# Layer norm row sums on GpSimd, a new order of the pieces, and a one-lane last pass, in a kernel of two interleaved attention layers

## The chip, the cores and the metric

The kernel runs on one core of one Trainium2 chip. The metric is device time in microseconds (us), the median of several executions; lower is better. Engines are named as in the profile: PE is TensorE's matmuls, PEld its weight loads, DVE is VectorE, ACT is ScalarE, POOL is GpSimd, SP is the engine whose queue issues the weight DMAs.

## The reference

Four residual blocks over 2048 rows of width 640: a recurrent attention layer with memory (A), a local dilated attention layer (B), and both once more with the same weights. Each takes a layer norm of its input.

```
x = x + A(layernorm(x))       # 64 segments of 32 rows, 8 memory rows carried from one to the next
x = x + B(layernorm(x))       # each row attends to 8 rows, two apart
x = x + A(layernorm(x))
x = x + B(layernorm(x))

def A(x):                     # 32 heads of 192
    for s in segments:
        h = concat(mem, x[s])                  # 8 + 32 rows
        q, k, v = h@Wq, h@Wk, h@Wv
        o = (softmax(mask(q k^T / sqrt(192))) v) @ Wo
        mem, out[s] = o[:8], o[8:]
```

## The kernel before

The rows lie in the free dimension, the 640 features in 5 chunks of 128 partitions. The four blocks run as one pipeline: in step t the first A layer works on segment t (lane 0) and the second A layer on segment t-2 (lane 1). Both use the same weights, so a full step has 2 x 40 = 80 columns in each A matmul and 2 x 32 = 64 in each B matmul. There are 66 A steps, of which the first two and the last two have one lane, and a last pass of B alone. `ORDER` lists the pieces of a step; each piece's instructions go to their engines in this order. Capital letters are layer A (K3: the k projection of head group 3; KE3: its eviction; S, E, EM, PO, R, OT: scores, exponential, mask, attention product, reciprocal, normalised output; Oa3, Ob3: output projection halves), small ones layer B, and `L...` the norm for the next step. 79 of the 128 weight pieces stay on chip; 49 are streamed in each step, from a ring of 8 buffers.

```python
ORDER = """
K0 Q0 bsq K0y QE0 KE0 V0 bst bmv VE0 Q1 S0 ... br bap ...
... OT15 E7 OT25 LSQ PO6 EM7 Oa2 R6 T7 Ob2 Oa3 TE7
Ob3 OT16 OT26 Oa5 PO7 Oa6 R7 lst LMV Ob5 Oa4 Ob6 OT17 LR OT27 Ob4 LAP O7x O7y MEMa O7z MEMb X1
"""                                            # [most of it cut]
LAST = "bsq bst bmv br bap bq bqE bk bkE bs0 be0 bv bs1 be1 eb0 bvE bt eb1 btE bp0 on0 bp1 on1 bo boE by byE"

def ln_sq(self, x):                            # bsq, LSQ: sums over the 5 chunks
    nc.vector.tensor_tensor(out=sq, in0=x, in1=x, op=mult)
    for j, v in enumerate((x, sq)):            # 128x64 <- 128x320, twice
        nc.vector.tensor_reduce(out=s[:, j, :], in_=v.rearrange("p c n -> p n c"), op=add, axis=X)
    nc.vector.tensor_copy(out=hl[:, 0], in_=s)                   # high part, bf16
    nc.vector.tensor_tensor(out=hl[:, 1], in0=s, in1=hl[:, 0], op=subtract)   # low part

def ln_stats(self, hl):                        # bst, lst: sum over the partitions by a ones matmul
    for j in range(2): nc.tensor.matmul(ps, lhsT=ones, rhs=hl[:, j], ...)
# ln_mv (bmv, LMV): mean and variance on DVE; ln_r (br, LR): 1/sqrt as exp(-0.5 ln) on ACT

def ln_big(self, x, mr, dst):                  # bap, LAP
    nc.vector.tensor_tensor(out=xc, in0=x, in1=m, op=subtract)   # 128x320
    for l in range(2):
        nc.vector.tensor_tensor(out=dst[:, :, l, :], in0=xc[lane l], in1=r[lane l], op=mult)

def mem_out(self, t, g):                       # MEMa, MEMb: memory rows from PSUM to the next step's input
    nc.vector.tensor_copy(out=h[..., 0:NM], in_=acc_lanes(g)[..., 0:NM])

def b_x1(self, b):                             # X1: x + A(...), from PSUM, in two halves
    nc.vector.tensor_tensor(out=x1, in0=acc, in1=xin, op=add)
# x_take: GpSimd copies the next segment's rows into xin
```

The softmax here doesn't subtract the row's maximum and nothing guards it: scores larger than these inputs give would overflow.

Of the kernel before, what the change touches and what calls it, by code (L numbers as in the profile page):

```python
# [11 lines left out]
F32 = mybir.dt.float32  # L12
ACT = mybir.ActivationFunctionType
# [4 lines left out]
P = 128  # L18
# [26 lines left out]


ORDER = """
K0 Q0 bsq K0y QE0 KE0 V0 bst bmv VE0 Q1 S0 K1 T0 QE1 br bap E0 TE0 KE1 V1 S1 EM0 Q3 PO0 VE1 QE3 E1 bq T1 R0 K2
KE2 bqE TE1 Q2 K3 V2 QE2 OT10 S2 KE3 bk EM1 OT20 S3 PO1 VE2 E2 bkE Q4 T2 EM2 bs1 E3 QE4 V3 R1 K4 TE2 be1 VE3
Q5 OT11 OT21 KE4 PO2 R2 EM3 T3 eb1 bs0 be0 V4 QE5 Oa0 VE4 bv TE3 OT12 OT22 bvE Q6 S4 PO3 eb0 E4 bt R3 QE6 btE  # L50
K5 T4 EM4 K6 KE5 TE4 bp0 V5 OT13 Ob0 OT23 KE6 on0 S5 bp1 VE5 PO4 T5 Oa1 E5 R4 on1 TE5 V6 bo Q7 EM5 OT14 S6 boE
OT24 VE6 Ob1 E6 QE7 PO5 T6 EM6 TE6 by byE R5 K7 KE7 V7 S7 VE7 OT15 E7 OT25 LSQ PO6 EM7 Oa2 R6 T7 Ob2 Oa3 TE7
Ob3 OT16 OT26 Oa5 PO7 Oa6 R7 lst LMV Ob5 Oa4 Ob6 OT17 LR OT27 Ob4 LAP O7x O7y MEMa O7z MEMb X1
""".split()


LAST = """
bsq bst bmv br bap bq bqE bk bkE bs0 be0 bv bs1 be1 eb0 bvE bt eb1 btE bp0 on0 bp1 on1 bo boE by byE
""".split()

def half_order():

    order = []
    for n in ORDER:
        if n[0] in "KQV" and len(n) == 2:
            order += [(n[0].lower(), int(n[1]), 0), (n[0].lower(), int(n[1]), 1)]
        elif n[:2] in ("Oa", "Ob"):
            order.append(("o", int(n[2]), int(n[1] == "b")))
        elif n == "O7x":
            order += [("o", 7, 0), ("o", 7, 1)]  # L70
    assert len(set(order)) == len(order) == 8 * NQUAD
    return order

def half_blocks(kind, i, h):

    if kind == "o":
        if i == NQUAD - 1:
            blocks = [(m, c) for c in range(NC) for m in O_ROWS[0] + O_ROWS[1]]
        else:
            blocks = [(m, c) for rows in O_ROWS for m in rows for c in range(NC)]  # L80
    elif (kind, i) == ("k", 0):
        blocks = [(c, n) for c in range(NC - 1) for n in range(6)] + [(NC - 1, n) for n in range(6)]
    else:
        blocks = [(c, n) for n in range(6) for c in range(NC)]
    return blocks[15 * h:15 * (h + 1)]
# [4 lines left out]
def resident_pieces():  # L90

    at, t = {}, 0.0
    for n in ORDER:
        if n[0] in "KQV" and len(n) == 2 and n != "K0":
            at.update({(n[0].lower(), int(n[1]), h): t + 15 * h for h in range(2)})
        elif n == "K0":
            at.update({("k", 0, h): t + 15 * h for h in range(2)})
        elif n[:2] in ("Oa", "Ob"):
            at[("o", int(n[2]), int(n[1] == "b"))] = t
        elif n == "O7x":  # L100
            at.update({("o", 7, h): t + 15 * h for h in range(2)})
        t += 30 if len(n) == 2 and n[0] in "KQV" else 15 if n[0] == "O" and n[1] in "ab" else 30 if n == "O7x" else NO_WEIGHTS.get(n.rstrip("01234567"), 0)
    pieces = [(at[u] + 8 * q, u + (q,)) for u in half_order() for q in range(2)]
    pieces.sort()
    stream, n_s = set(), len(pieces) - N_RES
    k = 0
    for j in range(n_s):
        want = (j + 0.5) * t / n_s
        while k < len(pieces) - (n_s - j) and abs(pieces[k + 1][0] - want) <= abs(pieces[k][0] - want):
            k += 1  # L110
        stream.add(pieces[k][1])
        k += 1
    return {u for _, u in pieces} - stream

class Kernel:
    def __init__(self, ctx, tc, xT, m0T, wA, wqkv, wo, out):

        self.tc = tc
        self.nc = tc.nc
        self.x = xT  # L120
        self.mem0 = m0T
        self.wA = wA
        self.b_src = (wqkv, wo)
        self.out = out
        self.n_seg = 2 * xT.shape[0]
        pool = lambda name, bufs, **kw: ctx.enter_context(tc.tile_pool(name=name, bufs=bufs, **kw))
        self.cp = pool("consts", 1)
        self.wres = pool("wres", 1)
        self.wring = pool("wring", RING)
        self.ap1 = pool("act1", 1)  # L130
        self.ap2 = pool("act2", 2)
        self.bp = pool("bact", 1)
        self.xp = pool("xio", 1)
        self.ps_one = pool("ps_one", 1, space=PSUM)
        self.units = {}
        self.place = {u: n for n, u in enumerate(half_order())}
        self.resident = resident_pieces()
        self.cur = {}
        self.n_big = 0
        self.xt, self.ots, self.qxs, self.kp, self.qp, self.vp, self.tp = {}, {}, {}, {}, {}, {}, {}  # L140
        self.x_load(0)
        self.build_consts()
# [148 lines left out]
    def span_of(self, t):  # L291

        self.l0 = 0 if t < self.n_seg else 1
        self.l1 = 2 if t >= LAG else 1
        self.cs = slice(LT * self.l0, LT * self.l1)

    def proj(self, ps, kind, i, h, t, chained=False):

# [131 lines left out]
    def a_o7(self, part):  # L430

        for k in {"x": range(18), "y": range(18, 24), "z": range(24, 30)}[part]:
            self.o_mm(NQUAD - 1, k // 15, k % 15)

    def acc_lanes(self, g):

        return self.acc[g][:, 0:(3 - g) * NT].rearrange("p (c l n) -> p c l n", l=2, n=LT)
# [18 lines left out]
    def ln_sq(self, x):  # L456

        nc = self.nc
        sq = self.bp.tile([P, NC, NX], BF16, name="sq", tag="sq")
        nc.vector.tensor_tensor(out=sq[:], in0=x[:], in1=x[:], op=ALU.mult)  # L460
        s = self.bp.tile([P, 2, NX], F32, name="ln_s", tag="xc")
        for j, v in enumerate((x, sq)):
            nc.vector.tensor_reduce(out=s[:, j, :], in_=v[:].rearrange("p c n -> p n c"), op=ALU.add, axis=mybir.AxisListType.X)
        hl = sq[:].rearrange("p c n -> p (c n)")[:, 0:4 * NX].rearrange("p (j a n) -> p j a n", j=2, a=2)
        nc.vector.tensor_copy(out=hl[:, 0], in_=s[:])
        nc.vector.tensor_tensor(out=hl[:, 1], in0=s[:], in1=hl[:, 0], op=ALU.subtract)
        return hl

    def ln_stats(self, hl):
        nc = self.nc  # L470
        ps = self.big("ps_st")
        for j in range(2):
            nc.tensor.matmul(ps[:, 0:2 * NX], lhsT=self.ones[:], rhs=hl[:, j].rearrange("p a n -> p (a n)"), start=(j == 0), stop=(j == 1))  # L473
        return ps

    def ln_mv(self, ps):

        nc = self.nc
        m = self.bp.tile([P, NX], F32, name="ln_m")
        nc.vector.tensor_scalar(out=m[:], in0=ps[:, 0:NX], scalar1=1.0 / D, scalar2=None, op0=ALU.mult)  # L480
        v = self.bp.tile([P, NX], F32, name="ln_v")
        nc.vector.tensor_tensor(out=v[:], in0=m[:], in1=m[:], op=ALU.mult)
        nc.vector.scalar_tensor_tensor(out=v[:], in0=ps[:, NX:2 * NX], scalar=1.0 / D, in1=v[:], op0=ALU.mult, op1=ALU.subtract)
        return m, v

    def ln_r(self, mv):

        nc = self.nc
        m, v = mv
        nc.scalar.activation(out=v[:], in_=v[:], func=ACT.Ln, bias=self.eps_t[:])  # L490
        r = self.bp.tile([P, NX], F32, name="ln_r")
        nc.scalar.activation(out=r[:], in_=v[:], func=ACT.Exp, scale=-0.5)
        return m, r

    def ln_big(self, x, mr, dst):
# [1 line left out]
        nc = self.nc  # L497
        m, r = mr
        xc = self.bp.tile([P, NC, NX], F32, name="ln_xc", tag="xc")
        nc.vector.tensor_tensor(out=xc[:], in0=x[:], in1=m[:].unsqueeze(1).to_broadcast([P, NC, NX]), op=ALU.subtract)  # L500
        for l in range(2):
            nc.vector.tensor_tensor(out=dst[:, :, l, :], in0=xc[:, :, SEG * l:SEG * (l + 1)],
                                    in1=r[:, SEG * l:SEG * (l + 1)].unsqueeze(1).to_broadcast([P, NC, SEG]), op=ALU.mult)

# [22 lines left out]
    def b_kE(self, b):  # L527

        o = SEG * (b % 2)
        for l in range(2):  # L530
            k = self.bkp[:, 0:NC * NX].rearrange("p (c l n) -> p l c n", c=NC, l=2)[:, l]
            self.nc.vector.tensor_tensor(out=self.KX[:, :, l, :, o:o + SEG], in0=k.unsqueeze(2).to_broadcast([P, NC, 2, SEG]),
                                         in1=self.par_mask[:].unsqueeze(3).to_broadcast([P, NC, 2, SEG]), op=ALU.mult)
# [1 line left out]
    def b_qE(self):  # L535

        self.qx = self.bp.tile([P, NC, BPC, NX], BF16, name="QX", tag="xc")
        q = self.bqp[:, 0:NC * NX].rearrange("p (c n) -> p c n", c=NC)
        self.nc.vector.tensor_tensor(out=self.qx[:], in0=q.unsqueeze(2).to_broadcast([P, NC, BPC, NX]),
                                     in1=self.pair_mask[:].unsqueeze(3).to_broadcast([P, NC, BPC, NX]), op=ALU.mult)  # L540

    def b_v(self):
        nc = self.nc
# [195 lines left out]
    def a_piece(self, n, t):  # L739
        if n == "K0":  # L740
            return self.k0(t)
        if n == "K0y":
            return self.k0y()
        if n[:2] == "O7":
            return self.a_o7(n[2])
        if n == "X1":
            return self.b_x1(t)
        k, i = n[:-1], int(n[-1])
# [12 lines left out]
    def step(self, t):  # L761
# [3 lines left out]
        nt = t + 1  # L765
        if a:
            self.span_of(t)
        if 1 < nt < self.n_seg:
            self.x_take(nt)
        for n in ORDER if a else LAST:  # L770
# [82 lines left out]
```

## Time and profile before

| | before |
|---|---|
| time, median of 3 | 3138.72 us (3137.41 to 3142.72) |
| profiled span | 3138.8 us |
| PE busy | 3063.2 us, 98% |
| DVE, ACT, POOL busy | 75%, 56%, 2% |
| median step, row-sum matmul of B's norm to the next step's | 46.44 us |
| first x1 addition of the last rows to the end ("tail") | 21.15 us |

The timeline of the kernel before shows one boundary between two steps: start, length, engine, source line, operation, tiles, shapes, count, and in brackets how long the engine had been idle and what ended that.

```profile
1488.27 0.47 ACT L390 ACTIVATE R<-R 128x320 f32<-128x320 f32 x1
...
1488.78 0.49 DVE L408 TENSOR_TENSOR OT<-ps_o,R 128x320 bf16<-128x320 f32 x1
...
1489.18 0.31 DVE L413 TENSOR_TENSOR OT<-ps_o,R 64x160 bf16<-64x160 f32 x1
...
1489.50 0.32 DVE L414 TENSOR_TENSOR OT<-ps_o,R 64x160 bf16<-64x160 f32 x1
...
1489.85 0.49 DVE L500 TENSOR_TENSOR ln_xc<-xin_88,ln_m 128x320 f32<-128x320 bf16 x1
...
1490.45 0.56 DVE L502 TENSOR_TENSOR hT_92<-ln_xc,ln_r 128x160 bf16<-128x160 f32 x2
...
1490.74 0.42 PE L420 MATMUL ps_acc_49872<-OT,w_o_11_1962 128*128 128x80 bf16 x7
1490.93 0.20 DVE L454 CAST hT_92<-ps_acc_49871 128x48 bf16<-128x48 f32 x1
1491.18 0.45 PE L303 MATMUL ps_k<-hT_92,w_k_00_386 128*128 128x80 bf16 x8
...
1491.97 0.42 POOL L655 COPY xin_86<-XT_49165 128x160 bf16<-128x160 bf16 x1 [46.01 <-DVE x_369 L510]
...
1492.12 0.71 DVE L463 TENSOR_REDUCE ln_s<-x_369 128x64 f32<-128x320 bf16 x1
```

Seven output matmuls start at 1490.74; at 36 ns each the eighth place would be 1490.99, and the first K matmul starts at 1491.18, 0.19 us late. No idle time is shown for it, because the modelled length of a matmul (about 0.2 us here) covers such a wait. It can only be found from the starts. Behind it stands a serial chain on DVE with no gap over 0.11 us: OT products, the norm's subtraction and multiplications, and the copy of the memory rows.

### The profile page before, as it was taken

What the parts mean: (1) busy time and instruction counts of PE and PEld (TensorE: products, weight loads), DVE (VectorE), ACT (ScalarE), POOL (GpSimd) and SP (SyncE); (2) the same over time, 40 slices, a digit from 0 to 9 for tenths busy, and PEclk for the clock granted to TensorE, in tenths of its full rate; (3) what the DMA queues carried; (4) which work ended last, traced back from release to release, by engine and by line L of the source; (5) the groups of instructions that cost most, each with busy time, mean ns of one, the idle gap of its engine ahead of it and who ended that gap; (6) DMA issues with size and microseconds to landing.
All of it is one profiled execution on the core that took longest, in us unless ns stands there. A gap on an engine that the chain in (4) does not pass through costs nothing.

```text
span 3138.8 us, 185804 instructions
## 1 busy us (share of the span) xinstructions
PE 3063.2 (98%) x83160; PEld 3036.4 (97%) x83160; DVE 2358.2 (75%) x6883; ACT 1747.2 (56%) x3829; POOL 48.2 (2%) x162
## 2 busy tenths in 40 slices
PE   6899999999999999999999999999999999999996
PEld 5799999999999999999999999999999999999996
DVE  3577777777777777777777777777777777777775
ACT  2355556555556556556555655555655655655653
POOL 2000000000000000000000000000000000000000
PEclk6899999999999999999999999999999999999998
DMA  9988888888888888888888888888888888888885
GB/s 360 320 263 267 263 262 265 264 264 265 266 268 263 268 266 263 268 266 263 268 266 261 267 263 267 261 265 268 263 267 266 264 267 267 263 269 266 262 274 184
DMA packets 487807, 838.02 MB, mean 267 GB/s; under 512 B 54240, under 2 KB 261984, under 8 KB 487008
## 3 DMA queue, kind: packets, MB, share of 16 engines
q1 hardware_dynamic: 477648, 820.89, 83.2%
q8 instruction: 651, 10.67, 1.4%
q10 hardware_dynamic: 9360, 5.26, 0.6%
q14 instruction: 148, 1.21, 0.1%
HBM read 823.31 MB, written 2.62 MB: 263 GB/s over the span
## 4 chain that ended last, share of the span: by engine, by line
PE 95%; DMA 3%; issue 1%; DVE 1%; ACT 0%; SPq 0%; DVEq 0%; ACTq 0%
PE ps_k L303 18%; PE ps_q L303 18%; PE ps_v L303 18%; PE ps_vt L349 6%; PE ps_o L401 5%; PE ps_s L368 5%; PE ps_by L634 2%; PE ps_bq L523 2%; PE ps_bv L548 2%; PE ps_bk L523 2%; DMA w_ring<-in_wA_dram 1%; PE ps_bs L575 1%; PE ps_bo L598 1%; PE ps_bvt L561 1%; PE ps_st L473 0%
## 5 line engine op out<-in xcount | busy, mean ns | idle before, releaser
L303 PEld LDWEIGHTS <-w_ring 128*128 128x128 bf16 x17754 | 784.4, 100 | 19.4 <-DMA w_ring<-in_wA_dram 10.5
L388 ACT ACTIVATE R<-ps_o 64x320 f32<-64x320 f32 (+1 forms) x1056 | 448.5, 425 | 273.8 <-PE ps_o L401 223.6
L342 ACT CAST VT_140<-ps_v 128x480 bf16<-128x480 f32 (+1 forms) x528 | 288.9, 547 | 230.7 <-PE ps_v L303 227.6
L329 ACT CAST KF_121<-ps_k 128x480 bf16<-128x480 f32 (+1 forms) x264 | 144.1, 546 | 391.2 <-PE ps_k L303 383.3
L374 ACT ACTIVATE Em<-ps_s 80x320 bf16<-80x320 f32 (+1 forms) x528 | 223.3, 423 | 157.2 <-PE ps_s L368 110.7
L420 PEld LDWEIGHTS <-w_ring 128*128 128x128 bf16 x6600 | 291.2, 100 | 3.5 <-DMA w_ring<-in_wA_dram 2.6
L335 DVE CAST QT_127<-ps_q 128x320 bf16<-128x320 f32 (+1 forms) x264 | 127.1, 481 | 203.4 <-PE ps_q L303 203.4
L357 DVE COPY Vt_134<-ps_vt 80x512 bf16<-80x512 bf16 x528 | 219.2, 415 | 71.5 <-PE ps_vt L349 69.3
L349 PE MATMUL ps_vt<-ident,VT_140 128*128 128x128 bf16 x3168 | 267.7, 221 | 0.0
L408 DVE TENSOR_TENSOR OT<-ps_o,R 128x320 bf16<-128x320 f32 (+1 forms) x528 | 249.9, 473 | 22.3 <-ACT R L390 16.6
L329 ACT CAST KF_123<-ps_k 128x480 bf16<-128x480 f32 (+1 forms) x264 | 144.1, 546 | 205.6 <-PE ps_k L303 203.9
L390 ACT ACTIVATE R<-R 128x320 f32<-128x320 f32 (+1 forms) x528 | 244.0, 462 | 16.6
L401 PE MATMUL ps_o<-Em,Vt_134 80*128 80x80 bf16 (+1 forms) x4224 | 238.0, 199 | 1.4 <-issue 1.3
L335 DVE CAST QT_125<-ps_q 128x320 bf16<-128x320 f32 (+1 forms) x264 | 126.5, 479 | 143.1 <-PE ps_q L303 71.9
L349 PEld LDWEIGHTS <-VT_140 128*128 128x128 bf16 x3168 | 191.5, 99 | 0.1
L303 PE MATMUL ps_q<-hT_92,w_ring 128*128 128x80 bf16 (+1 forms) x3234 | 185.8, 201 | 3.7 <-DMA w_ring<-in_wA_dram 2.6
L303 PE MATMUL ps_q<-hT_90,w_ring 128*128 128x80 bf16 (+1 forms) x3234 | 186.3, 201 | 2.2 <-DMA w_ring<-in_wA_dram 1.5
L401 PEld LDWEIGHTS <-Vt_134 80*128 80x128 bf16 x4224 | 181.6, 98 | 1.0 <-issue 0.7
L303 PE MATMUL ps_k<-hT_90,w_ring 128*128 128x80 bf16 (+1 forms) x3003 | 172.7, 201 | 1.4 <-DMA w_ring<-in_wA_dram 0.7
L303 PE MATMUL ps_k<-hT_92,w_ring 128*128 128x80 bf16 (+1 forms) x3003 | 171.8, 201 | 1.4 <-issue 1.4
L380 DVE TENSOR_TENSOR Em<-Em,maskA 80x320 bf16<-80x320 bf16 (+1 forms) x528 | 163.2, 309 | 12.5 <-ACT Em L374 8.4
L414 DVE TENSOR_TENSOR OT<-ps_o,R 64x160 bf16<-64x160 f32 (+1 forms) x528 | 165.1, 313 | 7.3
(3084 smaller groups left out, 8305.2 us busy)
## 6 DMA issues: line engine op xcount, KB each, us to landing
w_ring<-in_wA_dram SPq DMA_DIRECT2D x1716, 256.0 KB, 3.9
w_ring<-in_wA_dram SPq DMA_DIRECT2D x1518, 224.0 KB, 4.0
out_dram<-YT_94 ACTq DMA_DIRECT2D x32, 80.0 KB, 3.7
wqkv_sb<-in_wqkv_dram SPq DMA_DIRECT2D x3, 800.0 KB, 7.7
wo_sb<-in_wo_dram SPq DMA_DIRECT2D x1, 800.0 KB, 7.4
w_k_00_386<-in_wA_dram SPq DMA_DIRECT2D x1, 256.0 KB, 2.8
w_k_10_405<-in_wA_dram SPq DMA_DIRECT2D x1, 256.0 KB, 3.8
w_q_10_438<-in_wA_dram SPq DMA_DIRECT2D x1, 256.0 KB, 4.6
```

Of the source, the lines that this page charges most:

```text
L303: self.nc.tensor.matmul(ps[:, NT * n + c0:NT * n + c1], lhsT=self.block(kind, i, h, k), rhs=hT[:, NT * c + c0:NT * c + c1], start=(h == 0 ...
L329: self.nc.scalar.copy(out=kf[:, :, self.cs], in_=self.kp[i][:, 0:6 * NT].rearrange("p (a n) -> p a n", a=6)[:, :, self.cs])
L335: nc.vector.tensor_copy(out=qt[:, :, 0:4:3, cs], in_=pv[:, :, 0:3:2, cs])
L342: self.nc.scalar.copy(out=vt[:, :, self.cs], in_=self.vp[i][:, 0:6 * NT].rearrange("p (a n) -> p a n", a=6)[:, :, self.cs])
L349: nc.tensor.transpose(out=ps[:, n, :], in_=self.VT[:, NT * n:NT * n + P], identity=self.ident[:])
L357: nc.vector.tensor_copy(out=vt[:, :, 0:4:3, :], in_=src[:, :, 0:3:2, :])
L374: self.nc.scalar.activation(out=e[0:NT, :, cs], in_=self.sv[i][0:NT, :, cs], func=ACT.Exp, scale=float(DH) ** -0.5)
L388: self.nc.scalar.activation(out=r[rows, :, :, self.cs], in_=d, func=ACT.Ln)
L390: self.nc.scalar.activation(out=rf, in_=rf, func=ACT.Exp, scale=-1.0)
L401: nc.tensor.matmul(ov[:, pr, b, self.cs], lhsT=vt[0:NT, 512 * pr + P * b:512 * pr + P * (b + 1)], rhs=em[0:NT, 2 * pr + b // 2, self.cs], ...
L408: self.nc.vector.tensor_tensor(out=ot[:, :, 0:3:2, cs], in0=self.ov[:, :, 0:4:3, cs], in1=self.r[i][:, :, :, cs], op=ALU.mult)
L420: self.nc.tensor.matmul(self.acc[c // 3][:, o:o + self.cs.stop - self.cs.start], lhsT=self.block("o", i, h, k), rhs=ot[:, m, self.cs], sta ...
```

## The change

The intent: take one of the two reductions of each norm off DVE, by three adds on GpSimd; move pieces in the step, above all the last output chunks; and let the last pass of B, in which only lane 1 has rows left, work on that lane alone. The core of the diff; not shown are the same cut to `[:, ns]` in the other norm functions, and small helpers for the new pieces `O6x`, `O6y`:

```diff
 ORDER = """            # [cut]
-K0 Q0 bsq K0y QE0 KE0 V0 bst bmv VE0 Q1 S0 K1 T0 QE1 br bap E0 ...
-... Ob3 OT16 OT26 Oa5 PO7 Oa6 R7 lst LMV Ob5 Oa4 Ob6 OT17 LR OT27 Ob4 LAP O7x O7y MEMa O7z MEMb X1
+K0 K0y Q0 KE0 bsq V0 bst K1 QE0 S0 VE0 Q1 E0 KE1 bmv EM0 ...
+... OT15 OT25 PO6 Oa2 LSQ T7 Ob2 R6 EM7 Oa5 Oa3
+TE7 OT16 OT26 Ob3 PO7 Ob5 lst LMV Oa6 R7 O6x LR OT17 Oa4 Ob4 O6y OT27 LAP O7x O7y O7z MEMa MEMb X1
 LAST = """
-bsq bst bmv br bap bq bqE bk bkE bs0 be0 bv bs1 be1 eb0 bvE bt eb1 btE bp0 on0 bp1 on1 bo boE by byE
+bsq bst bmv br bap bk bkE bq bqE bv bs1 be1 bvE eb1 bt btE bp0 on0 bp1 on1 bo boE by byE
@@ half_blocks
+            if i == NQUAD - 2:      # second half of O6: by output chunk, 9 + 6 blocks
+                blocks = blocks[:15] + sorted(blocks[15:], key=lambda b: b[1])
@@ ln_sq
-        nc.vector.tensor_tensor(out=sq[:], in0=x[:], in1=x[:], op=ALU.mult)
-        for j, v in enumerate((x, sq)):
-            nc.vector.tensor_reduce(out=s[:, j, :], in_=v[:].rearrange("p c n -> p n c"), ...)
+        ns = self.b_rows()          # both lanes' columns, or the last lane's in the last pass
+        add = lambda out, a, b: nc.gpsimd.tensor_tensor(out=out, in0=a, in1=b, op=ALU.add)
+        add(s[:, 2:4, ns], x[:, 0:2, ns], x[:, 2:4, ns])
+        add(s[:, 2, ns], s[:, 2, ns], s[:, 3, ns])
+        add(s[:, 0, ns], s[:, 2, ns], x[:, 4, ns])
+        nc.vector.tensor_tensor(out=sq[:, :, ns], in0=x[:, :, ns], in1=x[:, :, ns], op=ALU.mult)
+        nc.vector.tensor_reduce(out=s[:, 1, ns], in_=sq[:, :, ns].rearrange("p c n -> p n c"), ...)
@@ step
+        else:                       # the last pass
+            self.bl = range(1, 2)
```

## The prediction

> **What bounds the kernel now.** The matmul stream. The page has PE busy 98% and 95% of the chain of waits; the windows view of 328.7 to 2985 us has PE 2650.5 of 2656.3 us at clock 1.00, VectorE 77%, GpSimd under 1%. In the timeline a 128x80 matmul starts every 36 ns, a 128x128 transpose every 56 ns. The Trainium skill, "TensorE: Matmul & The Clock Gate", section "Wait — 56ns, not 53.3ns?", gives N/2.4 GHz + 2.5 ns: 35.8 and 55.8; the trace agrees. A step's matmuls at these spacings sum to about 46.2 us; undisturbed steps take 46.44, the mean 46.6: hidden waits are about 0.4 us a step. The one repeated wait, about 0.19 us, is a step's first K matmul waiting for memory rows, which VectorE copies after the last OT products and the norm's apply. Outside lie a DMA-filled start (DMA share about 1.0 to 105 us) and a tail from 3117.6 us, a serial chain, partly at half clock.
>
> **What the change does.**
> 1. It takes one 0.70 us reduction (128x64<-128x320) off VectorE per norm, two a step, but VectorE is not the limit. Three GpSimd adds replace it. Estimate: small GpSimd instructions in the trace cost about 0.18 us; the skill's "GPSIMD Engine Reference", section 3.1, gives about 2.6 cycles per element for two inputs, so at 1.2 GHz the adds take 0.45, 0.3 and 0.3, together 0.9 to 1.1 us; no run here shows that rate yet. After the x1 adds GpSimd first copies the next x rows (0.42 us), so the sum is ready about 1.5 us after x1; VectorE's square and two reductions took 1.6. The cast on VectorE waits for GpSimd, so the row-sum matmul gets its data when it did (slack about 0.3 us). Hence 0 per step, perhaps +0.1.
> 2. The reordering keeps every matmul. Summing measured spacings along both orders, the distances that matter stay: x1 to row sums 3.2 us, last attention product to its output chunks 2.8, norm sums to next K 3.2; PSUM reuse distances stay over about 1.2. The moved output chunks leave the chain to the first K as it was. Gain 0 to 0.05 us per step, 0 to 3 us; DMA noise +-5.
> 3. The last norm and local attention on one lane: the norm chain from x1 to h2T, 5.2 us, becomes about 4.0; QX (1.49) and KX (0.88) halve, one score group, two of four exponentials (2.41 to 1.2) and one mask (0.69) go. The projections stay (1.5 us each at half clock) and hide much of this. Net 2 to 3 us off the tail.
>
> **Prediction.** 3138.7 - 2.3 (tail) - 1.5 (steady) = about 3135 us; range 3122 to 3149. Faster by over 2%: 0.01; within 2%: 0.96; slower by over 2%: 0.03.
>
> **What would show it.** Median step still 46.4 us; PE 98%; VectorE busy down by about 90 us, GpSimd up by 100 to 150 us; adds of about 0.4, 0.3, 0.3 us; the first K still waiting about 0.2 us; last x1 add to end 2 to 3 us shorter.
>
> **What would make it wrong.** GpSimd adds of 2 us in all, or slowed by VectorE's memory traffic: the row-sum matmuls then stall (0.5 us a step would cost 33 us). A PSUM buffer reused too early in the new order. A step-1 stall on the local weights, now needed in another order. Conversely, if the hidden 0.4 us per step goes, about 25 us are gained.

## More of the kernel before

The page of the kernel before: the first line gives busy time by engine, then come the granted PE clock in 40 slices (9 is 90% or more), the DMA queue that carries instructions, and the chain of work that ended last.

```profile
PE 3063.2 (98%) x83160; PEld 3036.4 (97%) x83160; DVE 2358.2 (75%) x6883; ACT 1747.2 (56%) x3829; POOL 48.2 (2%) x162
...
PEclk6899999999999999999999999999999999999998
...
q8 instruction: 651, 10.67, 1.4%
...
PE 95%; DMA 3%; issue 1%; DVE 1%; ACT 0%; SPq 0%; DVEq 0%; ACTq 0%
```

The matmul stream is nearly the whole time, and from the third slice to the last but one its clock is the full one or nearly so.

## The result, and the profile after

| | before | after |
|---|---|---|
| time, median of 3 | 3138.72 us | 3135.9 us (3131.49 to 3136.4) |
| profiled span | 3138.8 us | 3128.9 us |
| DVE busy; sum of its instructions' times | 2358.2; 2648.6 us | 2322.0; 2559.5 us |
| POOL busy | 48.2 us | 188.8 us |
| median step | 46.44 us | 46.44 us |
| sum of 60 full steps | 2796.1 us | 2794.1 us |
| tail | 21.15 us | 19.10 us |

The ratio is 0.9984, with a 95% interval of 0.9961 to 1.0007.

The page of the kernel after:

```profile
PE 3060.0 (98%) x83155; PEld 3035.9 (97%) x83155; DVE 2322.0 (74%) x6748; ACT 1741.9 (56%) x3827; POOL 188.8 (6%) x558
...
q8 instruction: 651, 10.67, 1.4%
...
PE 95%; DMA 3%; issue 1%; DVE 1%; ACT 0%; SPq 0%; POOL 0%; POOLq 0%; DVEq 0%; ACTq 0%
```

And the timeline of the kernel after, at a boundary between two steps. Lines are picked from those of about 4 us.

```profile
1487.40 0.56 DVE L523 TENSOR_TENSOR hT_92<-ln_xc,ln_r 128x160 bf16<-128x160 f32 x2
...
1487.69 0.42 PE L428 MATMUL ps_acc_49760<-OT,w_o_11_1966 128*128 128x80 bf16 x7
1487.88 0.20 DVE L467 CAST hT_92<-ps_acc_49759 128x48 bf16<-128x48 f32 x1
1488.13 0.45 PE L311 MATMUL ps_k<-hT_92,w_k_00_388 128*128 128x80 bf16 x8
...
1488.86 0.47 POOL L682 COPY xin_86<-XT_49357 128x160 bf16<-128x160 bf16 x1 [8.99 <-DVE x_371 L531]
...
1489.29 0.43 POOL L475 TENSOR_TENSOR ln_s<-x_371 128x128 f32<-128x128 bf16 x1
...
1489.80 0.32 POOL L475 TENSOR_TENSOR ln_s<-ln_s 128x64 f32<-128x64 f32 x1
...
1490.19 0.31 POOL L475 TENSOR_TENSOR ln_s<-ln_s,x_371 128x64 f32<-128x64 f32 x1
...
1490.54 0.23 DVE L482 CAST sq<-ln_s 128x128 bf16<-128x128 f32 x1 [0.63 <-POOL ln_s L475]
...
1490.80 0.29 DVE L483 TENSOR_TENSOR sq<-ln_s,sq 128x128 bf16<-128x128 f32 x1
...
1491.35 0.28 PE L490 MATMUL ps_st<-sq,ones 128*128 128x128 bf16 x2
```

The reader should see three things. The first K matmul is late as before: 1487.69 + 7 x 0.036 = 1487.94, and it starts at 1488.13. The three adds run after the copy of the next rows, 0.43, 0.32 and 0.31 us. And DVE, freed of a reduction, stands idle 0.63 us for the last of them: it starts nothing else in that time. The subtraction ends at 1491.09, 0.26 us before the row-sum matmul, which follows the stream without a wait.

The two profiles differ by 9.9 us, the medians by 2.8. The profiled execution of the kernel after was the fastest of its three. The experiments have to say what part of this belongs to the change.

### The profile page after: what moved, and what is told of

Read it like the earlier page. It is cut to its first block, busy times and chain, and to the rows that moved or that the text cites. A ratio compares the mean times of both kernels' runs of the same rounds, so it can differ in the third digit from the quotient of the medians. Undisturbed runs are those within 1.5% of the kernel's fastest.

```text
span 3128.9 us, 186160 instructions
## 1 busy us (share of the span) xinstructions
PE 3060.0 (98%) x83155; PEld 3035.9 (97%) x83155; DVE 2322.0 (74%) x6748; ACT 1741.9 (56%) x3827; POOL 188.8 (6%) x558
## 3 DMA queue, kind: packets, MB, share of 16 engines
q8 instruction: 651, 10.67, 1.4%
## 4 chain that ended last, share of the span: by engine, by line
PE 95%; DMA 3%; issue 1%; DVE 1%; ACT 0%; SPq 0%; POOL 0%; POOLq 0%; DVEq 0%; ACTq 0%
PE ps_k L311 18%; PE ps_v L311 18%; PE ps_q L311 18%; PE ps_vt L357 6%; PE ps_o L409 5%; PE ps_s L376 5%; PE ps_bq L544 2%; PE ps_by L661 2%; PE ps_bk L544 2%; PE ps_bv L575 2%; PE ps_bs L602 1%; DMA w_ring<-in_wA_dram 1%; PE ps_bo L625 1%; PE ps_bvt L588 1%; PE ps_st L490 0%
## 5 line engine op out<-in xcount | busy, mean ns | idle before, releaser
L343 DVE CAST QT_129<-ps_q 128x320 bf16<-128x320 f32 (+1 forms) x264 | 127.1, 482 | 160.1 <-PE ps_q L311 160.1
L311 PE MATMUL ps_k<-hT_90,w_ring 128*128 128x80 bf16 (+1 forms) x3168 | 183.8, 201 | 3.1 <-DMA w_ring<-in_wA_dram 1.3
L311 PE MATMUL ps_k<-hT_92,w_ring 128*128 128x80 bf16 (+1 forms) x3168 | 182.9, 201 | 3.8 <-issue 2.1
L311 PE MATMUL ps_q<-hT_90,w_ring 128*128 128x80 bf16 (+1 forms) x3003 | 172.1, 201 | 2.3 <-DMA w_ring<-in_wA_dram 1.0
L311 PE MATMUL ps_v<-hT_90,w_ring 128*128 128x80 bf16 (+1 forms) x2937 | 170.5, 201 | 3.2 <-issue 1.4
L311 PE MATMUL ps_q<-hT_92,w_ring 128*128 128x80 bf16 (+1 forms) x3003 | 171.4, 201 | 1.2 <-DMA w_ring<-in_wA_dram 1.2
```

Source lines behind the costliest of these rows:

```text
L311: self.nc.tensor.matmul(ps[:, NT * n + c0:NT * n + c1], lhsT=self.block(kind, i, h, k), rhs=hT[:, NT * c + c0:NT * c + c1], start=(h == 0 ...
```

## The experiments

"First K late" is, over the 60 full steps, the median of the time by which a step's first K matmul starts later than 36 ns after the last output matmul. "Step" is the median distance of the row-sum matmuls of B's norm. Both come from the starts in the trace.

### The parts alone

Kernels of one batch share the runs of the kernel before on one chip, where its median was 3145.38 us.

`order_only`: the new order and the re-sorted output chunks only.

```diff
 # the kernel after, with
-        add(...)  x3 on nc.gpsimd
+        nc.vector.tensor_reduce(out=s[:, 0, ns], in_=x[:, :, ns].rearrange("p c n -> p n c"), ...)
-            self.bl = range(1, 2)      # and LAST as before
```

> The kernel before with only the new order of the pieces and the re-sorted last output chunks; row sums by VectorE reductions and both lanes in the last pass as before. Theory A (the gain of the change is the shorter tail alone; the steady step is set by the spacing of the matmuls and one wait of 0.19 us at the first K matmul, which no part of the change touches): median distance of the row-sum matmuls 46.44 us, first K still 0.19 us late in nearly every step, tail from the last x1 addition to the end 21.2 us as before, time within 3 us of before. Rival B (the new order is what gained): time 2 to 4 us below before, with a shorter median step or fewer late K matmuls.

Measured: 3140.35 us, ratio 0.9989 (0.9974 to 1.0004); step 46.44 us, first K late by 0.191 us, tail 20.99 us.

`pool_only`: the row sums on GpSimd only; `ORDER` and `LAST` as before.

```diff
 # the kernel before, with
-        nc.vector.tensor_reduce(out=s[:, 0, :], in_=x ...)
+        add(...)  x3 on nc.gpsimd
```

> The kernel before with only the row sums moved to GpSimd adds, old order, both lanes in the last pass. Theory A: VectorE's summed instruction time falls by about 92 us and the time does not follow: median step 46.44 us, the row-sum matmul gets its data about 0.1 us later than in the kernel before and still does not wait; tail shorter by 0.3 to 0.5 us; time within 3 us of before. Rival C (VectorE's freed time is what gained): median step shorter by 0.05 us or more, time 3 us or more below before.

Measured: 3144.36 us, ratio 1.0002 (0.9984 to 1.0019); step 46.44 us, first K late by 0.192 us; the sum of DVE's instruction times fell from 2648.6 to 2558 us, the time did not follow. The tail was 21.51 us, no shorter; the expected 0.3 to 0.5 us did not come, though the norm's chain in it was 0.17 us shorter (4.95 us against 5.12).

`lane_only`: the one-lane last pass only, with DVE reductions.

```diff
 # the kernel before, with
+            self.bl = range(1, 2)      # in the last pass, LAST as in the change
+        ns = self.b_rows()             # the norm's instructions on [:, ns]
```

> The kernel before with only the last pass of the local layer cut to one lane (VectorE reductions over half the columns, old order elsewhere, the shortened last list). Theory A: median step 46.44 us, tail from the last x1 addition to the end 19.0 to 19.6 us against 21.2, so 1.6 to 2.1 us gained, nearly all of the change's gain; time 1 to 3 us below before. Rivals B and C: less than 0.5 us gained here.

Measured: 3139.53 us, ratio 0.9992 (0.9973 to 1.0011); step 46.44 us, tail 18.32 us, shorter than the 19.0 to 19.6 expected and than that of the whole change; the granted clock after its norm was 0.65, against 0.61 in the first profile of the change.

`after_again`: the whole change.

> The changed kernel once more, on the same chip as its three parts. Theory A: its gain over before is that of the one-lane pass plus 0.3 to 0.5 us, 2 to 3 us in all, with tail about 19.1 us; the 9.9 us between the two first profiles was mostly luck in waits that the profile calls issue, and does not come again. If those 9.9 us belong to the change, the profiled span here is again 8 us or more below that of before.

Measured: 3140.37 us, ratio 0.9991 (0.9976 to 1.0006). The profiled span was 3144.4 us; the kernel before, on the same chip, had spans of 3139.0 to 3146.6 us, with a median of 3143.6. So the 9.9 us did not come again. The 60 full steps took 2803.2 us here and 2794.1 us in the first profile of the same kernel: luck of this size hides parts of 2 us. By times alone no part is told from zero.

What follows by the traces: no part moves the step or the late first K, so rivals B and C fall for the step. DVE's freed time buys nothing. The tail is where a part shows.

### The tail

The timeline of the kernel before, from the last x1 additions to the first B projection:

```profile
3117.65 0.26 DVE L510 TENSOR_TENSOR x_369<-ps_acc_106721,xin_88 128x96 bf16<-128x96 f32 x1 [2.77 <-PE ps_acc_106721 L420]
...
3118.55 0.68 DVE L463 TENSOR_REDUCE ln_s<-x_369 128x64 f32<-128x320 bf16 x1
3119.15 0.68 DVE L463 TENSOR_REDUCE ln_s<-sq 128x64 f32<-128x320 bf16 x1
3119.86 0.23 DVE L465 CAST sq<-ln_s 128x128 bf16<-128x128 f32 x1
...
3122.21 0.56 DVE L502 TENSOR_TENSOR h2T_371<-ln_xc,ln_r 128x160 bf16<-128x160 f32 x2 [0.30 <-ACT ln_r L492]
```

The kernel after:

```profile
3109.84 0.26 DVE L531 TENSOR_TENSOR x_371<-ps_acc_106749,xin_88 128x96 bf16<-128x96 f32 x1 [0.60 <-PE ps_acc_106749 L428]
...
3110.51 0.31 POOL L475 TENSOR_TENSOR ln_s<-x_371 128x64 f32<-128x64 bf16 x1 [40.25 <-DVE x_371 L531]
...
3110.90 0.25 POOL L475 TENSOR_TENSOR ln_s<-ln_s 128x32 f32<-128x32 f32 x1
3111.23 0.24 POOL L475 TENSOR_TENSOR ln_s<-ln_s,x_371 128x32 f32<-128x32 f32 x1
3111.51 0.20 DVE L482 CAST sq<-ln_s 128x64 bf16<-128x64 f32 x1 [0.41 <-POOL ln_s L475]
...
3113.53 0.33 DVE L523 TENSOR_TENSOR h2T_373<-ln_xc,ln_r 128x160 bf16<-128x160 f32 x1 [0.42 <-ACT ln_r L512]
```

`lane_only`, the same chain without GpSimd:

```profile
3117.55 0.41 DVE L474 TENSOR_REDUCE ln_s<-x 128x32 f32<-128x160 bf16 x1
3117.88 0.41 DVE L475 TENSOR_REDUCE ln_s<-sq 128x32 f32<-128x160 bf16 x1
3118.32 0.20 DVE L477 CAST sq<-ln_s 128x64 bf16<-128x64 f32 x1
```

From the first x1 addition to the cast it is 2.21 us before, 1.67 after and 1.50 in `lane_only` (whose first addition, not shown, starts at 3116.83). At half the columns a DVE reduction takes 0.41 us, while three dependent adds on GpSimd take 1.0 us from start to end; DVE waits for them 0.41 us. So in the last pass the GpSimd part costs about 0.17 us of what the one lane gains. To the norm's result it is 5.12 us before, 4.01 after, 3.85 in `lane_only`.

The rest of the tail depends on the granted clock, and on where in the tail it falls. The next four lines are the windows view of the tail of the kernel before, of `order_only` (whose last pass is the old one), of the kernel after and of a later run of it (`after_third`, below), in this order. The column before the DMA share is the granted clock.

```profile
3117.65:3138.80 21.15, 8.79 (x149) 7.36 (x146) 10.33 (x26) 3.82 (x8) 0.00 (x0) 0.58 0.02 5
```

```profile
3119.24:3140.23 20.99, 8.59 (x149) 7.25 (x145) 10.33 (x26) 3.82 (x8) 0.00 (x0) 0.69 0.02 5
```

```profile
3109.84:3128.90 19.06, 8.17 (x144) 7.09 (x140) 7.23 (x22) 2.58 (x6) 0.80 (x3) 0.69 0.02 5
```

```profile
3115.00:3134.90 19.90, 8.95 (x144) 7.73 (x140) 7.23 (x22) 2.58 (x6) 0.80 (x3) 0.58 0.02 5
```

The next two are the stretch from the norm's result to the end, in the kernel before and in the kernel after.

```profile
3122.78:3138.80 16.02, 7.90 (x136) 6.88 (x135) 6.18 (x13) 3.21 (x6) 0.00 (x0) 0.61 0.02 6
```

```profile
3113.86:3128.94 15.08, 7.53 (x131) 6.71 (x130) 4.53 (x11) 2.03 (x4) 0.00 (x0) 0.61 0.02 5
```

The mean clock of a whole tail does not make two tails comparable. `order_only` has 0.69 and the kernel before 0.58, yet their tails differ by only 0.16 us: the kernel before had the half clock all through the norm, where the matmuls are few. After the norm's result both took about 16.0 us, and in both the clock was full for 3.4 us, from 3.2 us after that result, and half otherwise. In the first profile of the kernel after, the full clock came at nearly the same place, 3.3 us after the norm's result, and this stretch took 15.08 us. So at the same clock in the same place the change takes 0.9 us off this stretch, and 1.0 to 1.1 us off the norm's chain (4.98 us in `order_only`, 5.12 before, 4.01 after): about 1.9 us in all, 20.99 us in `order_only` against 19.10. `after_third` had the half clock all through the stretch, which took 15.87 us. No profile of the old last pass has that state, so its 19.88 us cannot be set against the 21.15, although both tails have a mean of 0.58.

### Where the 0.19 us come from

Three kernels, in a batch where the kernel before had 3136.98 us.

`xc_early`: put the row-sum matmul a little earlier, and its mean, variance and subtraction of the mean on DVE before the last reciprocal is waited for.

```diff
-... Oa5 Oa3 TE7 OT16 OT26 Ob3 PO7 Ob5 lst LMV Oa6 R7 O6x LR OT17 ... OT27 LAP
+... Oa5 Oa3 lst TE7 OT16 OT26 LMV LXC Ob3 PO7 Ob5 Oa6 R7 O6x LR OT17 ... OT27 LAP
+        elif n == "LXC":
+            self.axc = self.ln_xc(x, self.amv[0])     # the subtraction, taken out of LAP
```

> The changed kernel, with the next step's row-sum matmul put a little earlier, its mean and variance and the subtraction of the mean done on VectorE before it waits for the last reciprocal, so that only the multiplications stand between the last OT products and the copy of the memory rows. Theory A (the 0.19 us by which the first K matmul comes late in nearly every step is VectorE's serial chain OT products, apply of the norm, memory copy): the late first K falls from about 0.19 us to under 0.05 in the full steps, median step 46.25 us, 10 to 13 us less than the changed kernel, about 0.9955 of before. Rival D (the first K waits for its weights or for the matmul unit itself): still 0.19 us, step 46.44.

Measured: 3128.31 us, ratio 0.9965 (0.9945 to 0.9985); first K late by 0.034 us, step 46.26 us. Rival D falls. In time this is some 6 us below the change, by the ratios, where 10 to 13 were expected; the other stalls of its profile came to 13.6 us (see below), and the interval includes the expected ratio of 0.9955.

`mem_act`: only the copies of the memory rows on ScalarE.

```diff
-            nc.vector.tensor_copy(out=h[:, :, ls, 0:NM], in_=a[:, :, ls, 0:NM])
+            nc.scalar.copy(out=h[:, :, ls, 0:NM], in_=a[:, :, ls, 0:NM])
```

> The changed kernel, with only the two copies of the memory rows from PSUM moved from VectorE to ScalarE, which is idle there. Theory A: the apply of the norm, which the first K matmul needs too, still ends where it did, so the late first K falls only to 0.08 to 0.15 us, 2 to 7 us gained over the changed kernel. If the copy alone were the limit, the wait would be gone, 11 us gained. Rival D: no change.

Measured: 3129.96 us, ratio 0.998 (0.9964 to 0.9996); first K late by 0.077 us, step 46.34 us. The copy is one link, the end of the norm's apply the other, as expected; the 2 to 7 us are not shown, as the interval includes the ratios of the change itself.

`xc_mem`: both.

> Both of the two: subtraction of the mean earlier, and memory rows copied by ScalarE. Theory A: no late first K, median step 46.22 to 46.27 us, no better than the earlier subtraction alone by more than 3 us. Rival D: 46.44 us.

Measured: 3125.16 us, ratio 0.9957 (0.9935 to 0.998); first K late by 0.023 us, step 46.23 us. The median is 3.2 us under that of `xc_early`, where no more than 3 was expected, a difference well inside the intervals.

### How much room the GpSimd adds have

`pool_slow`, in the same batch: two useless adds behind the three of B's norm.

```diff
         add(s[:, 0, ns], s[:, 2, ns], x[:, 4, ns])
+        if x is getattr(self, "x1", None):
+            for _ in range(2):
+                add(s[:, 0, ns], s[:, 2, ns], x[:, 4, ns])
```

> The changed kernel with two more, useless GpSimd adds (0.31 us each, 0.40 start to start) behind the three of the second layer's norm; the result stays right. Theory A says that the three adds are hidden, but only by about 0.25 us (the subtraction on VectorE ends 0.25 us before the row-sum matmul starts): with 0.8 us more the row-sum matmul waits 0.4 to 0.6 us in each step, median step 46.8 to 47.1 us, 25 to 40 us more in all. Rival E (GpSimd's adds have ample room, as GpSimd is 6% busy): no more than 3 us.

Measured: 3161.91 us, ratio 1.0076 (1.0061 to 1.0091), with a step of 46.93 us, 0.49 us longer. The timeline of `pool_slow` at the row-sum matmul:

```profile
1502.01 1.07 POOL L475 TENSOR_TENSOR ln_s<-ln_s,x 128x64 f32<-128x64 f32 x3
...
1503.12 0.23 DVE L485 CAST sq<-ln_s 128x128 bf16<-128x128 f32 x1 [1.38 <-POOL ln_s L475]
...
1503.38 0.29 DVE L486 TENSOR_TENSOR sq<-ln_s,sq 128x128 bf16<-128x128 f32 x1
1503.40 0.54 PE L493 MATMUL ps_st<-sq,ones 128*128 128x128 bf16 x2
```

The two matmuls now stretch over 0.54 us, as the second waits for the subtraction. GpSimd is busy 6% of the span in the kernel after and still a quarter of a microsecond from being the limit; rival E falls. The page's share says nothing about that, the slack at the consumer does.

### What the luck is, and a faster version

`best`: the kernel after with both edits of `xc_mem`, and in the last pass the row sums by DVE.

```diff
+        if len(self.bl) == 2:
             add(...)  x3 on nc.gpsimd
+        if len(self.bl) == 1:
+            nc.vector.tensor_reduce(out=s[:, 0, ns], in_=x[:, :, ns].rearrange("p c n -> p n c"), ...)
```

> The changed kernel with the earlier subtraction, the memory rows copied by ScalarE, and, in the last one-lane pass only, both row sums again by VectorE reductions over half the columns. Theory A: median step 46.2 to 46.25 us as in the run of the two together; norm chain of the tail from x1 to h2T 3.85 us as in the one-lane kernel without GpSimd, against 4.0 in the changed kernel; tail 18.3 to 19.4 us, the clock's state being the rest; time 11 to 15 us below before, 8 to 12 below the changed kernel.

Measured: 3118.87 us beside 3135.16 for the kernel before, ratio 0.9944 (0.9932 to 0.9956); that is 16.3 us less, where 11 to 15 were expected. Step 46.23 us, first K late by 0.022 us, x1 to the norm's result 3.84 us. The tail was 19.41 us, with the half clock all through the stretch after the norm, as in `after_third`. The timeline of `best` at a boundary:

```profile
1480.47 0.48 DVE L523 TENSOR_TENSOR ln_xc<-xin,ln_m 128x320 f32<-128x320 bf16 x1
...
1482.94 0.56 DVE L533 TENSOR_TENSOR hT<-ln_xc,ln_r 128x160 bf16<-128x160 f32 x2
...
1483.72 0.42 PE L428 MATMUL ps_acc<-OT,w_o 128*128 128x80 bf16 x7
1483.74 0.20 ACT L467 CAST hT<-ps_acc 128x48 bf16<-128x48 f32 x1 [1.38 <-PE ps_acc L428]
...
1483.99 0.45 PE L311 MATMUL ps_k<-hT,w_k 128*128 128x80 bf16 x8
```

The first K starts at 1483.99, where 1483.72 + 7 x 0.036 = 1483.97 would be on time; the subtraction starts 2.5 us before the multiplications, instead of 0.6 us in the kernel after, in time that DVE had spent waiting.

`after_third`: the change once more, 5 rounds, on the same chip.

> The changed kernel, beside the best one on the same chip, for a closer interval of the change itself. Theory A: 2 to 5 us below before (ratio 0.9984 to 0.9994), first K late by 0.19 us, median step 46.44 us, tail 19.0 to 19.8 us.

Measured: 3131.46 us, ratio 0.9984 (0.9969 to 0.9999); step 46.44 us, first K late by 0.192 us, tail 19.88 us, just above the range expected. So the change does seem to gain, by 0.1 to 0.2%: the three batches gave 0.9984, 0.9991 and 0.9984, though only this interval leaves out 1, and barely. `best` is 12.6 us below it, just more than the 8 to 12 expected.

`stream_more`: fewer weights kept on chip. It asks what the waits are that the profile calls issue.

```diff
-N_RES = 79
+N_RES = 73
```

> The changed kernel with 73 instead of 79 weight pieces kept on chip, so 55 instead of 49 pieces are streamed in each step (12% more), result right. Theory F (the waits called issue, one possible place each 127.6 matmuls, are late 16 KB packets of TensorE's instruction stream, and they come late because the weight stream keeps the DMA engines busy): the sum of stalls over 0.15 us in the 60 full steps, other than the first K, rises from 7 to 15 us to over 25 us, the one-lane steps lengthen too, and the time grows by 15 us or more, with no waits on weights. Rival G (the packets' lateness does not depend on the weight stream): stalls as before, time within 5 us of the changed kernel. If the stream itself becomes the limit, the waits name the weights instead.

First what led to it. Apart from the first K, the full steps hold some 15 to 40 stalls of more than 0.15 us in an execution, at other places each time, 6 to 16 us in all. In the one-lane steps they come one after another. Here is the timeline of the kernel before, in the first of its last two A steps:

```profile
3035.22 0.80 PE L523 MATMUL ps_bq<-h2T_371,wqkv_sb 128*128 128x64 bf16 x22
...
3036.92 0.26 PE L523 MATMUL ps_bq<-h2T_371,wqkv_sb 128*128 128x64 bf16 x3 [0.90 <-issue]
```

It stops inside one group of matmuls whose data have all long been there. Numbering the matmuls of that execution, this stall and the five after it come before matmuls 80764, 80891, 81019, 81147, 81274 and 81402: 127 or 128 apart. The page shows 651 packets and 10.67 MB in the instruction queue, that is 16.4 KB each, and 83160 matmuls / 651 = 127.7. In the full steps of the kernel before, all 29 such stalls end 1.0 to 1.9 us after the end of one of these packets (median 1.43); by chance about a fifth would. The stalls are late blocks of TensorE's own instructions. The Trainium skill, "Runtime: NRT & Kernel Launch", section "Instruction fetch mechanics", says that the sequencer streams its instructions in 16 KiB blocks of 256 through its own DMA queue; a matmul with its weight load is two, so 128 matmuls. The trace agrees on the block.

Measured: 3184.17 us, ratio 1.014 (1.012 to 1.0161). The stalls other than the first K grew from 8.7 us (`after_third`) to 46.7 us in the 60 full steps, and 85 of 91 end 1.0 to 1.9 us after an instruction packet. The packets themselves take no longer (median 0.96 and 0.97 us): they start later, at the median by about 50 matmuls, counting the matmuls begun when a packet starts. So Theory F holds in its main point: a heavier weight stream delays the instruction stream. It is not clean, since some waits on weights appear too, against the expectation, and 25 of the 91 stalls fall on the first matmul of a streamed piece. These 25 hold about 14 us, so at most that much of the 46.7 us is weights; the others hold over 30 us, against under 8 in `after_third`.

## Why the prediction was right or wrong

The forecast was 3135 us, measured 3135.9, inside the range. That the number fits to 0.9 us is luck: the interval of the ratio reaches from 12 us less than before to 2 us more, the 1.5 us of the steady steps were not found, and the range of 3122 to 3149 us holds the old time too. What the runs test is the mechanism, term by term.

- *The matmul stream bounds the kernel; undisturbed steps take 46.44 us.* Right. In six executions of the change and its parts the step stayed 46.44 us. The Trainium skill, "TensorE: Matmul & The Clock Gate", section "Wait — 56ns, not 53.3ns?", gave the spacing, and the trace shows 36 ns at 80 columns.
- *A late first K of 0.19 us, by DVE's chain, which the change leaves as it is.* Right. It is there in each part, and two edits of that chain take it away, about 10 us over the run.
- *GpSimd's adds: 0.45, 0.3, 0.3 us, hidden, with about 0.3 us of slack.* Right: 0.43, 0.32, 0.31 and 0.26 us of slack. The cost per column is near that of the Trainium skill's "GPSIMD Engine Reference", section 3.1, whose 2.6 cycles per element are, by estimate, 2.17 ns at 1.2 GHz: halving the columns in the last pass saved 2.2 ns per column in the second add (0.32 to 0.25 us), but 1.9 in the first and the third. `pool_slow` shows that the slack is real and small.
- *"VectorE busy down by about 90 us".* The step that failed. The instructions' times summed fell by 89 us, as costed, but busy fell by 36. Busy counts time in which at least one instruction runs, and neighbours on DVE overlap, so an instruction taken out gives back less than its length: in `pool_only` busy fell from 2358.2 to 2294.6, 64 us. And the new order alone, with the same instructions, raised busy to 2388.4, 30 us, by spreading them out. The two and the last pass's 3 us make the 36. It cost the forecast nothing, as DVE is not the limit.
- *Tail 2 to 3 us shorter.* Nearly right: about 1.9 us at the same clock in the same place, and 2.05 between the first two profiles. The norm chain fell from 5.1 to 4.0 us as costed, and what follows it by 0.9 us. GpSimd's three adds cost 0.17 us of it, as `lane_only` shows. That the three projections now stand before the scores may cost something too; no run tests it.
- *Order: 0 to 3 us.* Not shown by time; `order_only` has 0.9989 with an interval that includes 1. One trace reading speaks for a small gain: from the last row-sum matmul of the recurrent steps to the last x1 addition, in the step paced by instruction blocks, the three profiles of the old order took 40.4 to 42.8 us, the nine of kernels with the new order's step 38.2 to 40.6 (leaving out `stream_more`). The one-lane step before it shows nothing of the kind: from its row-sum matmul to the next, 44.1 to 44.7 us in the old order and 42.7 to 46.3 in the new. Which move would do it was not tried. With the tail's 1.9 us this would account for most of the 3 to 5 us measured, but that sum is argued, not shown.

## What to carry to other kernels

When the matmuls already stand shoulder to shoulder, moving work off another engine gains nothing unless that work is in the chain that the next matmul waits for; look for that chain in the matmuls' start times, as a wait of 0.2 us hides inside a modelled matmul and shows as no idle time. Judge a helper engine by the slack at its consumer, not by its busy share, and don't put three dependent small adds on it where one reduction at half width is quicker. Where an effect is a tenth of a per cent, read it from a fixed stretch of the trace, since whole runs differ by more, and compare stretches that had the same granted clock in the same place: two tails here had the same mean of 0.58 and were still not alike.

## What the Trainium skill lacked or had wrong

- "Runtime: NRT & Kernel Launch", section "Instruction fetch mechanics", holds that instruction fetch is hidden by the sequencer's issue. Here it is not for TensorE: with matmuls of 40 columns a stall of about 0.5 to 2 us came at nearly each block of 127.7 matmuls, and with 12% more weight DMA traffic the stalls in 60 full steps grew from 8.7 to 46.7 us, of which at most about 14 us are waits on weights.
- "TensorE: Matmul & The Clock Gate", section "Back-to-back issue gap", gives about 81 ns per matmul at 128 columns for a stream of weight load and matmul pairs. Here such pairs stand 56 ns apart at 128 columns and 36 ns at 80, the spacing that the page gives for the matmul alone.
- "GPSIMD Engine Reference", section 3.1, gives the cost per element but no fixed cost for short instructions (section 2.1 of the page has only tens of cycles for one step of the dispatch). Here an add of 32 columns took 0.24 to 0.25 us and one of 64 took 0.31 to 0.32 us, about 0.18 us of it fixed, and dependent adds started 0.33 to 0.5 us apart.
